# Attention scores read from PSUM by the top-32 search, and expert sums on ScalarE and GpSimd

## The chip, the cores and the metric

The kernel runs on one core of one Trainium2 chip. The metric is the device time of one execution in microseconds (us); the time before is the median of three runs. The core has TensorE (PE in the profile, its weight loads PEld), VectorE (DVE), ScalarE (ACT), GpSimd (POOL) and the queue engine SyncE (SP). Each takes its instructions strictly in the order in which they were issued, so an instruction that waits holds all those behind it on its engine.

## What is computed

Attention that keeps the 32 largest scores of every row, and behind it a mixture of four experts on every token.

```python
scores = q @ k.T / 8                       # 2 batches x 8 heads, 576 x 576, 64 deep
kth    = 32nd largest score of each row
attn   = exp(scores - max) where scores >= kth else 0
attn  /= attn.sum(-1) + 1e-9
x      = concat over heads(attn @ v)       # 1152 tokens x 512
p      = domain_probs / (domain_probs.sum(-1) + 1e-9)
out    = sum over e of p[:, e] * (relu(x @ w1[e]) @ w2[e])     # 512 -> 1024 -> 512
```

All is float32. The matmuls get near that precision by splitting each operand into two float16 parts, HI and LO, and adding three products.

## The kernel before

The 1152 rows are cut into ten tiles: per batch four of 128 rows and one rest of 64. The 64-row rest of batch 0 comes first. A unit is one tile and one head (in a rest tile a pair of heads), so there are 72 units, numbered 0 to 71 here: 4, then 8 for each full tile, then 4.

What a unit does, in order:

- `emit_qk` (L596): four matmuls on PE give 128 x 576 scores in two PSUM banks, 288 columns each (`ps0`, `ps1`).
- `emit_scopy` (L617): ScalarE copies both halves into an SBUF tile `s`, of which there are four. The banks are then free for the next unit.
- `topk_op` (L623): seven steps on VectorE find the 32 largest. MAX8 gives the eight largest; MATCH_REPLACE overwrites them with a very small number in the work tile `w`; four rounds. The first search and the first replacement read `s`, the others `w`. Between consecutive steps of one unit stand steps of the next.
- `emit_exp` (L666): ScalarE writes exp of `s` into `w`, behind the last search.
- `emit_mask` (L670): for units 0 to 19 (tiles marked `d` in `MASKS`) VectorE does compare and multiply in one instruction (L675). For units 20 to 71 (`b`) VectorE writes the comparison as float16 over `s` (L679) and GpSimd multiplies it into `w` (L681).
- `emit_a` (L683): ScalarE makes the HI part and GpSimd the LO part, both in the tile `s`; `emit_at` transposes them by a DMA; `emit_av` (L702) multiplies by V into a PSUM bank `av`, one for four heads.
- `emit_x_half` (L736) divides by the row sums on VectorE, and `emit_x_end` makes the float16 parts of x.

The experts (`moe`, L821) run per tile: for each expert and each half of the 1024 hidden columns, 48 or 96 first-layer matmuls into a bank `m1`, the float16 parts of the hidden rows on ScalarE and GpSimd (`h_hi`, `h_lo`, which pass through one SBUF tile `hf`), and 12 or 24 second-layer matmuls (L915) into a bank `m2`, which gathers one expert's whole output. `evac` (L918) scales that output by the token's weight and sums the experts in `acc`: ScalarE writes the first expert's, VectorE adds the others (L935). The eight PSUM banks are two for scores, two `av`, two `m1`, two `m2`. Weights are loaded, scaled and split once, during the first 160 us.

Nothing in the loops sets the order: each step is an event with places taken from the table `ISSUE`, one number for each part of the step, and the events are issued by rising place (L1131). The table is written out by hand or by a planner, and decides where every instruction stands on every engine.

## Time and profile before

| | us |
|---|---|
| median of 3 runs | 584.38 |
| lowest and highest | 582.45, 586.53 |
| the profiled execution: its own time | 585.51 |
| its span, first to last instruction | 583.3 |
| busy: PE, DVE | 518.1, 491.5 |
| busy: ACT, POOL | 376.4, 363.2 |

The profile is of one execution, whose time is 2.2 us longer than its span. Starts in the timeline count from the start of the span. Busy time of PE says little on how full it is, since matmuls overlap in the records: a row of 0.22 us can be followed by the next after 0.06 us. What tells is the distance from start to start.

### The profile page before, as it was taken

The page shows a single profiled execution, that of the slowest core. Times are in us where ns is not written, and L with a number is a line of the kernel's source. Part 1 is how long each engine was busy: PE and PEld are TensorE (multiplying, and loading weights), DVE is VectorE, ACT ScalarE, POOL GpSimd, SP SyncE. Part 2 cuts the span into 40 slices and gives each one's busy share as a digit, 9 for nine tenths or more (in the row PEclk, how much of TensorE's full clock was granted, in tenths as well). Part 3 has the DMA queues.
Part 4 walks back from the last instruction along what each step waited for, and adds up shares of the span by engine and source line. Part 5 has one row for each costly group of instructions (what it writes and reads, how often), then busy time and mean ns, then how long its engine had stood idle before and what let it go on. Part 6 is the DMA issues. An engine that isn't in the chain of part 4 may idle for free. (4 is left out here: it accounts for less than half of the span.)

```text
span 583.3 us, 16478 instructions
## 1 busy us (share of the span) xinstructions
PE 518.1 (89%) x6676; PEld 390.3 (67%) x6676; DVE 491.5 (84%) x1066; ACT 376.4 (65%) x755; POOL 363.2 (62%) x387
## 2 busy tenths in 40 slices
PE   6669462658899999999899999999999999999996
PEld 3459461646577687776678775876878686677683
DVE  2888998899999999999989999999999988780122
ACT  3878988898774755677787876566565646443301
POOL 1344997898765656768777876667575747435300
PEclk9768665757899999999999999999999999999999
DMA  7999877234224353445465454234323314212210
GB/s 180 360 241 341 129 188 228 44 74 72 49 49 78 65 81 71 89 81 124 105 108 114 88 99 96 51 81 78 60 62 63 74 26 81 39 21 39 43 30 10
DMA packets 140459, 57.05 MB, mean 98 GB/s; under 512 B 128864, under 2 KB 132064, under 8 KB 140384
## 3 DMA queue, kind: packets, MB, share of 16 engines
q1 hardware_dynamic: 138016, 53.38, 43.3%
q10 hardware_dynamic: 2368, 2.62, 1.4%
q8 instruction: 52, 0.85, 0.6%
q14 instruction: 23, 0.19, 0.1%
HBM read 24.14 MB, written 2.36 MB: 45 GB/s over the span
## 5 line engine op out<-in xcount | busy, mean ns | idle before, releaser
L876 PE MATMUL m<-xt,w 128*128 128x128 f16 (+1 forms) x1280 | 203.0, 217 | 1.3 <-POOL w L420 1.3
L915 PE MATMUL m<-w,h 128*128 128x512 f16 (+1 forms) x960 | 197.5, 383 | 0.0
L874 PE MATMUL m<-xt,w 128*128 128x128 f16 (+1 forms) x1120 | 182.2, 217 | 2.4 <-DVE h L897 1.5
L875 PE MATMUL m<-xt,w 128*128 128x128 f16 (+1 forms) x1120 | 182.0, 217 | 0.0
L633 DVE MAX8 m<-w 128x8 f32<-128x576 f32 x216 | 159.6, 752 | 2.8
L915 PEld LDWEIGHTS <-h 128*128 128x128 f16 (+1 forms) x960 | 84.1, 101 | 90.2 <-issue 2.6
L876 PEld LDWEIGHTS <-w 128*128 128x128 f16 x1280 | 126.1, 100 | 1.5 <-POOL w L420 1.5
L874 PEld LDWEIGHTS <-w 128*128 128x128 f16 x1120 | 110.4, 100 | 4.4 <-DVE h L897 1.7
L875 PEld LDWEIGHTS <-w 128*128 128x128 f16 x1120 | 110.4, 100 | 2.9 <-issue 1.0
L635 DVE MATCH_REPLACE8 w<-m,w 128x576 f32<-128x576 f32 x144 | 106.6, 742 | 0.0
L894 POOL TENSOR_TENSOR h<-hf,h 128x512 f16<-128x512 f32 x64 | 75.1, 1173 | 48.7 <-ACT h L885 29.7
L691 POOL TENSOR_TENSOR s<-w,s 128x512 f16<-128x512 f32 x68 | 78.7, 1159 | 36.6 <-ACT s L689 23.6
L681 POOL TENSOR_TENSOR w<-w,s 128x576 f32<-128x576 f32 x52 | 67.1, 1292 | 46.7 <-DVE s L679 43.6
L668 ACT ACTIVATE w<-s,nb,es 128x576 f32<-128x576 f32 x68 | 58.7, 865 | 28.5 <-DVE m L633 25.0
L620 ACT ACTIVATE s<-ps 128x288 f32<-128x288 f32 x144 | 51.1, 405 | 39.1 <-PE ps L613 14.8
L689 ACT ACTIVATE s<-w 128x576 f16<-128x576 f32 x68 | 46.2, 681 | 43.7 <-POOL w L681 36.4
L633 DVE MAX8 m<-s 128x8 f32<-128x576 f32 x72 | 53.9, 748 | 15.1 <-ACT s L620 15.0
L891 ACT ACTIVATE hf<-m 128x512 f32<-128x512 f32 x64 | 37.9, 592 | 31.5 <-PE m L876 15.9
L885 ACT ACTIVATE h<-m 128x512 f16<-128x512 f32 x72 | 42.1, 590 | 24.9 <-PE m L876 23.0
L729 PE MATMUL av<-vt,at 128*128 128x65 f16 (+1 forms) x1008 | 41.8, 199 | 15.6 <-DMA at<-s 15.6
L729 PEld LDWEIGHTS <-at 128*128 128x128 f16 (+1 forms) x1008 | 38.3, 103 | 23.9 <-DMA at<-s 18.1
L635 DVE MATCH_REPLACE8 w<-m,s 128x576 f32<-128x576 f32 x72 | 53.4, 741 | 0.0
(156 smaller groups left out, 807.3 us busy)
## 6 DMA issues: line engine op xcount, KB each, us to landing
w<-in_moe_w_dram SPq DMA_DIRECT2D x16, 1024.0 KB, 8.8
qraw<-in_q_dram SPq DMA_DIRECT2D x8, 256.0 KB, 4.5
qb<-qa SPq DMA_DIRECT2D x16, 128.0 KB, 2.5
out_dram<-o ACTq DMA_DIRECT2D x8, 256.0 KB, 2.3
at<-s SPq DMA_TRANSPOSE x68, 3.2
vraw<-in_v_dram SPq DMA_DIRECT2D x2, 512.0 KB, 5.3
kraw<-in_k_dram SPq DMA_DIRECT2D x4, 256.0 KB, 3.2
vraw<-in_v_dram SPq DMA_DIRECT2D x4, 256.0 KB, 4.2
```

The source lines that it names most:

```text
L620: ACT.activation(st[:, hf * 288:hf * 288 + 288], ps[:, 0:288], AF.Copy)
L633: DVE.max(m, s_t[u] if r == 0 else w_t[u])
L635: DVE.match_replace(w_t[u], m, s_t[u] if r == 0 else w_t[u], NEG)
L668: ACT.activation(w_t[u], s_t[u], AF.Exp, bias=nb, scale=es)
L681: POOL.tensor_tensor(w, w, g, op=OP.mult)
L691: POOL.tensor_tensor(a[:, 640:1152], w[:, 0:512], a[:, 0:512], op=OP.subtract)
L729: PE.matmul(o, lhsT=att[:, blk, ps], rhs=r, start=(i == 0), stop=(i == len(seq) - 1))
L874: PE.matmul(o, lhsT=HI[e, 0, c][:, fc], rhs=xs(0, c), start=(c == 0), stop=False)
L875: PE.matmul(o, lhsT=HI[e, 0, c][:, fc], rhs=xs(1, c), start=False, stop=False)
L876: PE.matmul(o, lhsT=LO[e, 0, c][:, fc], rhs=xs(0, c), start=False, stop=(c == 3))
L894: POOL.tensor_tensor(h[:, 1], hf, h[:, 0], op=OP.subtract)
L915: PE.matmul(y[z * 64:z * 64 + M, :], lhsT=h_t[es, qd][:, p // 2, h0:h0 + M], rhs=w, start=(fc == 0 and p == 0), stop=(fc == 7 and p == 2))
```

## The change

The copy `emit_scopy` is gone. A unit's scores now lie in one PSUM tile of two banks, and there are two such tiles, four banks in place of two. First search, first replacement, exponential and mask read them there; the mask is one VectorE instruction for all units, so that GpSimd no longer multiplies. To make room, `av` and `m2` have one bank each in place of two. The tile `a` of the float16 parts is a tile of its own, out of three; `w` has four tiles in place of three. For tiles 1 to 5 (`p` in `EVAC`) the sums of experts move: ScalarE scales the output into `yf`, which shares the single SBUF tile of `hf`, and GpSimd adds it. The small matrix `pmat` is halved and its matmul done in two parts. The table `ISSUE` is new throughout, so that all instructions stand in another order; of it two lines are shown.

```diff
@@ -43,184 +43,175 @@
-MASKS = 'dddbbbbbbb'
-
...
+EVAC = 'dpppppdddd'
...
 ISSUE = [
-    (1, 4), (2, 6), (5, 8), (28, 31), (37, 50), (11,), (16, 17), (20, 21, 26, 34), (44, 58, 78, 95),
...
+    (1, 3), (4, 5), (10, 11), (6, 9), (18, 26), (27,), (34, 35), (38, 41, 88, 119), (45, 52, 106, 113),
...
 ]
 C_QK, C_V0, C_X, C_W1, C_W2 = 11, 14, 5, 10, 14
 
@@ -240,8 +231,8 @@
     cp = pool("const", 1)
     wp = pool("weights", 1)
     kvp = pool("kv", 1)
-    sp_ = pool("s", 4)
-    wkp = pool("wk", 3)
+    sp_ = pool("s", 3)
+    wkp = pool("wk", 4)
     atp = pool("at", 2)
     rawp = pool("raw", 2)
     hlp = pool("hl", 1)
@@ -251,10 +242,10 @@
     hfp = pool("hf", 1)
     op_ = pool("o", 2)
     stp = pool("st", 2)
-    ps_s = pool("pss", 1, space=PSUM)
-    ps_av = pool("psav", 2, space=PSUM)
+    ps_s = pool("pss", 2, space=PSUM)
+    ps_av = pool("psav", 1, space=PSUM)
     ps_m1 = pool("psm1", 2, space=PSUM)
-    ps_m2 = pool("psm2", 2, space=PSUM)
+    ps_m2 = pool("psm2", 1, space=PSUM)
 
     events, known = [], []
 
@@ -283,7 +274,7 @@
     with tc.manual_schedule(engines={getattr(mybir.EngineType, x) for x in MANUAL}):
 
         ident = cp.tile([128, 128], F32, name="ident")
-        pmat = cp.tile([128, 128], F32, name="pmat")
+        pmat = cp.tile([128, 64], F32, name="pmat")
         ones = cp.tile([128, 128], F32, name="ones")
         invk = cp.tile([128, B, H], F32, name="invk")
         invv = cp.tile([128, B, H], F32, name="invv")
@@ -526,7 +517,8 @@
         for i, (t, x) in enumerate(units):
             first_of.setdefault(t, i)
             last_of[t] = i
-        sp_t, s_t, w_t, m_t, a_t, at_t, av_t = {}, {}, {}, {}, {}, {}, {}
+        s_t, w_t, m_t, a_t, at_t, av_t = {}, {}, {}, {}, {}, {}
+        HS = S // 2
 
         qF, kF = [None], {}
 
@@ -560,18 +552,24 @@
             kF[x] = sp_.tile([128, S], F32, tag="s", name="kf")
             copy_rows(kF[x], p0, p1)
 
+        def scores():
+
+            return ps_s.tile([128, 2, 512], F32, tag="s", name="ps0")
+
+        def rows2(w):
+            return w.rearrange("p (t n) -> p t n", t=2)
+
         def emit_qk_whole(u, x):
-            sp_t[u] = []
+            p = scores()
+            s_t[u] = p[:, :, 0:HS]
             for hf in range(2):
-                ps = ps_s.tile([128, 512], F32, tag=f"s{hf}", name=f"ps{hf}")
+                ps = p[:, hf, :]
                 for z in (slice(0, 64), slice(64, 128)):
                     PE.matmul(ps[z, 0:288], lhsT=qF[0][z, x * 64:x * 64 + 64], rhs=kF[x][z, hf * 288:hf * 288 + 288],
                               start=True, stop=True)
-                sp_t[u].append(ps)
 
         def emit_a_whole(u):
             w = w_t.pop(u)
-            s_t.pop(u)
             p0, p1 = bank(ps_m1, "m1"), bank(ps_m2, "m2")[:, 0:64]
             for c in range(4):
                 PE.transpose(p0[:, c * 128:c * 128 + 128], w[:, c * 128:c * 128 + 128], ident)
@@ -599,9 +597,10 @@
                 emit_qk_whole(u, x)
                 return
             ta, tb = qt_t[t]
-            sp_t[u] = []
+            p = scores()
+            s_t[u] = p[:, :, 0:HS]
             for hf in range(2):
-                ps = ps_s.tile([128, 512], F32, tag=f"s{hf}", name=f"ps{hf}")
+                ps = p[:, hf, :]
                 ks = slice(hf * 288, hf * 288 + 288)
                 if t[2] == 64:
                     for j, src in enumerate((ta, tb)):
@@ -612,13 +611,6 @@
                     for j, src in enumerate((ta, tb)):
                         PE.matmul(ps[:, 0:288], lhsT=src[:, x, :],
                                   rhs=kt[x].rearrange("p c n -> p (c n)")[:, ks], start=(j == 0), stop=(j == 1))
-                sp_t[u].append(ps)
-
-        def emit_scopy(u):
-            st = sp_.tile([128, S], F32, tag="s", name="s")
-            for hf, ps in enumerate(sp_t.pop(u)):
-                ACT.activation(st[:, hf * 288:hf * 288 + 288], ps[:, 0:288], AF.Copy)
-            s_t[u] = st
 
         def topk_op(u, o):
             if u >= NU or u < 0:
@@ -631,8 +623,10 @@
                 w_t[u] = wkp.tile([128, S], F32, tag="w", name="w")
             if o % 2 == 0:
                 DVE.max(m, s_t[u] if r == 0 else w_t[u])
+            elif r == 0:
+                DVE.match_replace(rows2(w_t[u]), m, s_t[u], NEG)
             else:
-                DVE.match_replace(w_t[u], m, s_t[u] if r == 0 else w_t[u], NEG)
+                DVE.match_replace(w_t[u], m, w_t[u], NEG)
 
         eb_t, es_t = {}, {}
 
@@ -665,27 +659,19 @@
 
         def emit_exp(u):
             es, nb = eb_t.pop(u)
-            ACT.activation(w_t[u], s_t[u], AF.Exp, bias=nb, scale=es)
+            ACT.activation(rows2(w_t[u]), s_t[u], AF.Exp, bias=nb, scale=es)
 
         def emit_mask(u):
             thr = m_t.pop(u)[:, 31:32]
-            sc, w = s_t[u], w_t[u]
-            mode = MASKS[tiles.index(units[u][0])]
-            if mode == "d":
-                DVE.scalar_tensor_tensor(w, sc, thr, w, op0=OP.is_ge, op1=OP.mult)
-            else:
-                g = sc.bitcast(F16).rearrange("p (t n) -> p t n", t=2)[:, :, 0:S // 2]
-                sc, w = (z.rearrange("p (t n) -> p t n", t=2) for z in (sc, w))
-                (DVE if mode == "b" else POOL).tensor_scalar(g, sc, thr, None, op0=OP.is_ge)
-                yield
-                POOL.tensor_tensor(w, w, g, op=OP.mult)
+            w = rows2(w_t[u])
+            DVE.scalar_tensor_tensor(w, s_t.pop(u), thr, w, op0=OP.is_ge, op1=OP.mult)
 
         def emit_a(u):
             if units[u][0] == tiles[0]:
                 yield from emit_a_whole(u)
                 return
             w = w_t.pop(u)
-            a_t[u] = a = s_t.pop(u).bitcast(F16)
+            a_t[u] = a = sp_.tile([128, S], F32, tag="s", name="a").bitcast(F16)
             ACT.activation(a[:, 0:576], w, AF.Copy)
             yield
             POOL.tensor_tensor(a[:, 640:1152], w[:, 0:512], a[:, 0:512], op=OP.subtract)
@@ -775,7 +761,8 @@
                 ACT.activation(hl.bitcast(BF16)[:, 0:n], x, AF.Square, accum_out=ss)
 
             def cross():
-                PE.matmul(cross_t[t], lhsT=pmat, rhs=st["ss"], start=True, stop=True)
+                for z in range(2):
+                    PE.matmul(cross_t[t][z * 64:z * 64 + 64], lhsT=pmat, rhs=st["ss"], start=True, stop=True)
 
             def total():
                 ss = st["ss"]
@@ -931,6 +918,11 @@
                 if e == order[0]:
                     acc[0] = op_.tile([128, DM], F32, tag="o", name="o")
                     ACT.activation(acc[0][0:M], yz, AF.Copy, scale=c[0:M])
+                elif EVAC[tiles.index(t)] == "p":
+                    yf = hfp.tile([128, 512], F32, tag="hf", name="yf")[0:M]
+                    ACT.activation(yf, yz, AF.Copy, scale=c[0:M])
+                    yield
+                    POOL.tensor_tensor(acc[0][0:M], acc[0][0:M], yf, op=OP.add)
                 else:
                     DVE.scalar_tensor_tensor(acc[0][0:M], yz, c[0:M], acc[0][0:M], op0=OP.mult, op1=OP.add)
                 if e == order[-1]:
@@ -977,9 +969,7 @@
 
         def make_pmat():
             for z in range(2):
-                for y in range(2):
-                    POOL.tensor_copy(pmat[z * 64:z * 64 + 64, y * 64:y * 64 + 64],
-                                     ident[z * 64:z * 64 + 64, z * 64:z * 64 + 64])
+                POOL.tensor_copy(pmat[z * 64:z * 64 + 64], ident[z * 64:z * 64 + 64, z * 64:z * 64 + 64])
 
         def norm_probs():
             for g, r0, n, m in ((0, 0, 128, 4), (4, 512, 64, 1), (5, S, 128, 4), (9, S + 512, 64, 1)):
@@ -1061,7 +1051,7 @@
 
         for u, (t, x) in enumerate(units):
             i = 10 * u
-            for what, fn in (("qk", emit_qk), ("scopy", emit_scopy), ("nb", emit_nb), ("exp", emit_exp),
+            for what, fn in (("qk", emit_qk), ("nb", emit_nb), ("exp", emit_exp),
                              ("mask", emit_mask), ("a", emit_a), ("at", emit_at)):
                 at(i + P[what + "_0" if t == tiles[0] and what != "at" else what], fn, u)
             at(i + P["av_first" if t == tiles[0] else "av_2" if u < P["av_n"] else "av"], emit_av, u)
```

Three places in the order. Names with numbers are buffers: `m` the eight largest, `w` the work tile, `s` the copy of the scores, `ps0` the scores in PSUM, `m2` an expert's output.

VectorE in the middle of the program before, at the first search of unit 42 and the masks of units 40 (`s_4827`) and 41 (`s_4926`):

```order
L633 MAX m_5170<-s_5144 128x8
L635 MATCH_REPLACE w_5176<-m_5170,s_5144 128x576
L679 TENSOR_SCALAR s_4827<-s_4827,m_4887 128x2x288
L281 RECIPROCAL qi_5059<-qps_5061 128x1
L633 MAX m_4981<-w_4997 128x8
L633 MAX m_5170<-w_5176 128x8
L635 MATCH_REPLACE w_5176<-m_5170,w_5176 128x576
L935 SCALAR_TENSOR_TENSOR o_4490<-m2_4983,pf_4005,o_4490 128x512
L633 MAX m_5170<-w_5176 128x8
L679 TENSOR_SCALAR s_4926<-s_4926,m_4981 128x2x288
L277 TENSOR_SCALAR kpt_5284<-m2_5235 128x2
L633 MAX m_5292<-s_5287 128x8
```

The same engine there now; `ps0_4838` are the scores of unit 41, `ps0_5002` of unit 42, `ps0_5127` of unit 43:

```order
L272 RECIPROCAL invv_115<-kps_4922 128x2
L625 MAX m_5007<-w_5009 128x8
L629 MATCH_REPLACE w_5009<-m_5007,w_5009 128x576
L667 SCALAR_TENSOR_TENSOR w_4845<-ps0_4838,m_4843,w_4845 128x576
L625 MAX m_5007<-w_5009 128x8
L272 RECIPROCAL invv_115<-kps_4779 128x2
L629 MATCH_REPLACE w_5009<-m_5007,w_5009 128x576
L268 TENSOR_SCALAR kpt_5135<-m2_5121 128x2
L625 MAX m_5007<-w_5009 128x8
L625 MAX m_5159<-ps0_5127 128x8
```

Before, the mask of unit 41 stood just ahead of the first search of unit 43, and each read its own SBUF tile. Now it reads the PSUM tile into which the scores of unit 43 go next, and between this mask and that search stand two searches, a replacement and two short instructions.

VectorE at the end of attention before, where `s_8750` are the scores of unit 71 and `s_8412` those of unit 69:

```order
L633 MAX m_8753<-s_8750 128x8
L635 MATCH_REPLACE w_8755<-m_8753,s_8750 128x576
L633 MAX m_8753<-w_8755 128x8
L635 MATCH_REPLACE w_8755<-m_8753,w_8755 128x576
L633 MAX m_8753<-w_8755 128x8
L635 MATCH_REPLACE w_8755<-m_8753,w_8755 128x576
L635 MATCH_REPLACE w_8661<-m_8659,w_8661 128x576
L633 MAX m_8659<-w_8661 128x8
L679 TENSOR_SCALAR s_8412<-s_8412,m_8479 128x2x288
L679 TENSOR_SCALAR s_8564<-s_8564,m_8659 128x2x288
L633 MAX m_8753<-w_8755 128x8
L679 TENSOR_SCALAR s_8750<-s_8750,m_8753 128x2x288
```

And now, where `ps0_8221` are the scores of unit 69 and `ps0_8415` those of unit 71:

```order
L625 MAX m_8332<-w_8349 128x8
L732 TENSOR_SCALAR r_8390<-av_8132 128x4
L733 RECIPROCAL r_8390<-r_8390 128x4
L737 TENSOR_TENSOR r_8390<-r_8390,invv_115 128x4
L738 TENSOR_TENSOR x_8070<-av_8132,r_8390 128x256
L667 SCALAR_TENSOR_TENSOR w_8349<-ps0_8221,m_8332,w_8349 128x576
L268 TENSOR_SCALAR xpt_8424<-xss_8409 128x1
L270 TENSOR_SCALAR xps_8425<-xpt_8424 128x1
L927 SCALAR_TENSOR_TENSOR o_7986<-m2_8357,pf_7595,o_7986 128x512
L625 MAX m_8459<-ps0_8415 128x8
```

The mask of unit 69 has moved from behind three of the last unit's rounds to ahead of its first search.

ScalarE in the middle before, with the two copies of the scores of unit 40 (`s_4827`) and unit 41 (`s_4926`); `hf` and `h` are hidden rows of an expert:

```order
L418 ACTIVATE vt0_139<-vraw_4715 128x5x64
L620 ACTIVATE s_4827<-ps0_4801 128x288
L620 ACTIVATE s_4827<-ps1_4804 128x288
L891 ACTIVATE hf_4889<-m1_4725 128x512
L418 ACTIVATE vt1_140<-vraw_4715 128x5x64
L668 ACTIVATE w_4674<-s_4545,nb_4834,es1_4807 128x576
L789 ACTIVATE x_4239<-x_4239,xps_4831 128x512
L791 ACTIVATE xhl_4791<-x_4239 128x512
L891 ACTIVATE hf_4908<-m1_4838 128x512
L620 ACTIVATE s_4926<-ps0_4896 128x288
L620 ACTIVATE s_4926<-ps1_4899 128x288
```

And now, at a sum of experts (`yf_4767`):

```order
L878 ACTIVATE hf_4743<-m1_4641 128x512
L761 ACTIVATE xhl_4746,xss_4747<-x_4257 128x512
L872 ACTIVATE h_4755<-m1_4641 128x512
L428 ACTIVATE kt6_137,kss_4762<-kraw_4691 128x320
L675 ACTIVATE a_4765<-w_4614 128x576
L923 ACTIVATE yf_4767<-m2_4715,pf_3827 128x512
L428 ACTIVATE kt7_138,kss_4762<-kraw_4691 128x320
L662 ACTIVATE w_4702<-ps0_4628,nb_4704,es1_4490 128x576
```

The pairs of copies (L620) are gone, and a scaling of an expert's output (L923) stands between the steps of the units.

## Rows read from the trace of the kernel before

**Rows 1.** The page, part 1: busy us (share of the span) and instructions.

```profile
PE 518.1 (89%) x6676; PEld 390.3 (67%) x6676; DVE 491.5 (84%) x1066; ACT 376.4 (65%) x755; POOL 363.2 (62%) x387
```

**Rows 2.** The windows view, three stretches: busy us of each engine, PEclk, DMA.

```profile
20.00:160.00 140.00, 94.33 (x1257) 77.06 (x1258) 127.49 (x281) 119.97 (x203) 106.83 (x80) 0.70 0.69 166
160.00:500.00 340.00, 334.55 (x4206) 251.66 (x4204) 326.46 (x704) 221.46 (x482) 230.71 (x265) 1.00 0.41 79
500.00:583.30 83.30, 78.45 (x1153) 55.10 (x1149) 28.71 (x60) 24.44 (x48) 23.93 (x24) 0.99 0.14 29
```

**Rows 3.** The page, part 4: the chain that ended last, by engine.

```profile
DVE 21%; PE 18%; issue 4%; POOL 3%; ACT 1%; DVEq 0%; POOLq 0%; ACTq 0%
```

**Rows 4.** Timeline of PE: start, us, what; scores of the last unit, what follows.

```profile
510.99 0.31 PE L609 MATMUL ps<-kt,qa 128*64 128x288 f16 x2
...
511.38 0.29 PE L609 MATMUL ps<-kt,qb 128*64 128x288 f16 x2
...
511.78 0.22 PE L874 MATMUL m<-xt,wx 128*128 128x128 f16 x1
...
512.28 0.22 PE L874 MATMUL m<-xt,wx 128*128 128x128 f16 x1
```

**Rows 5.** Pieces of the chain of waits: twelve second-layer matmuls; half a unit times V.

```profile
474.83 2.59 PE m L915 x12
477.42 0.44 PE av L729 x14
```

**Rows 6.** Timeline of all engines: the end.

```profile
578.49 1.53 DVE L935 SCALAR_TENSOR_TENSOR o<-m,pf,o 64x512 f32<-64x512 f32 x2 [3.65 <-PE m L915]
```

**Rows 7.** Groups of VectorE: out<-in, count, busy us, mean ns, idle before, releaser.

```profile
L679 DVE TENSOR_SCALAR s<-s,m 128x576 f16<-128x576 f32 x52 | 31.7, 611 | 10.4 <-ACT w L668 10.3
...
L675 DVE SCALAR_TENSOR_TENSOR w<-s,m,w 128x576 f32<-128x576 f32 x20 | 24.5, 1226 | 1.2 <-ACT w L668 1.2
...
L935 DVE SCALAR_TENSOR_TENSOR o<-m,pf,o 128x512 f32<-128x512 f32 x21 | 15.5, 738 | 17.0 <-ACT o L933 9.6 <-PE m L915 7.3
```

**Rows 8.** Timeline of VectorE: two masks of the first tiles.

```profile
113.11 0.81 DVE L675 SCALAR_TENSOR_TENSOR w<-s,m,w 128x576 f32<-128x576 f32 x1
...
124.05 2.21 DVE L675 SCALAR_TENSOR_TENSOR w<-s,m,w 128x576 f32<-128x576 f32 x1
```

**Rows 9.** Timeline of GpSimd at the same times.

```profile
115.63 2.13 POOL L420 TENSOR_TENSOR w<-w 128x1024 f16<-128x1024 f32 x1 [2.48 <-ACT w L418]
...
123.52 2.12 POOL L420 TENSOR_TENSOR w<-w 128x1024 f16<-128x1024 f32 x1
```

**Rows 10.** Timeline of VectorE: a replacement, then its own search, then another.

```profile
213.16 0.74 DVE L635 MATCH_REPLACE8 w<-m,w 128x576 f32<-128x576 f32 x1
...
213.94 0.76 DVE L633 MAX8 m<-w 128x8 f32<-128x576 f32 x1
...
219.42 0.74 DVE L635 MATCH_REPLACE8 w<-m,s 128x576 f32<-128x576 f32 x1
...
220.08 0.08 DVE L635 MATCH_VALUE_LOAD w<-m,w 128x8 f32 x1
```

**Rows 11.** Timeline of VectorE: first search of unit 71, mask of unit 69.

```profile
514.60 0.74 DVE L633 MAX8 m<-s 128x8 f32<-128x576 f32 x1
...
521.01 0.50 DVE L679 TENSOR_SCALAR s<-s,m 128x576 f16<-128x576 f32 x1
```

**Rows 12.** Waits of VectorE: us in total, times, longest us.

```profile
DVE m L633 <- ACT s L620: 15.0, 6, 9.8
...
DVE w L635 <- POOL s L693: 2.7, 2, 2.3
```

**Rows 13.** Timeline of PE: scores of unit 20.

```profile
155.45 0.30 PE L613 MATMUL ps<-kt,qa 128*128 128x288 f16 x1
```

**Rows 14.** Timeline of VectorE: mask of unit 18.

```profile
166.39 1.62 DVE L675 SCALAR_TENSOR_TENSOR w<-s,m,w 128x576 f32<-128x576 f32 x1
```

**Rows 15.** Groups of GpSimd: the same columns.

```profile
L681 POOL TENSOR_TENSOR w<-w,s 128x576 f32<-128x576 f32 x52 | 67.1, 1292 | 46.7 <-DVE s L679 43.6 <-DVE qps L279 1.8 <-DVE r L746 0.9
```

2 lines of the change are left out of this document (1 added, 1 removed), and 313 rows, old and new, of the table ISSUE.

## The prediction

> **What bounds the kernel now.** I read the windows first, then the chain of waits, then single engines. The windows cut the span at 160 and 500 us: in the middle stretch PE is busy 334.6 of 340 us at a granted clock of 1.00 and VectorE 326.5, while ScalarE and GpSimd have a third of the time free [rows 2]. In the first 140 us VectorE has 127 and PE only 94, at a mean granted clock of 0.70; in the last 83 PE has 78 and VectorE 29 [rows 2]. Over the span VectorE's 491.5 and PE's 518.1 lie far above the other two [rows 1], and the part of the chain that the page shares out is VectorE 21% and PE 18% against 1% of ScalarE and 3% of GpSimd [rows 3]. So two engines are full at once.
>
> PE's fullness must be checked by starts, since busy counts overlap. Nine first-layer matmuls take 0.50 us from start to start, 0.056 each [rows 4]; twelve of the second layer take 2.59, 0.216 each; 14 matmuls times V take 0.44 [rows 5]; a unit's scores take 0.5 [rows 4]. Between the scores of unit 20, at 155.45 [rows 13], and of unit 71, at 510.99 [rows 4], the order has 2688 first-layer and 696 second-layer matmuls and some 51 units: 2688 x 0.056 + 696 x 0.216 + 51 x 0.95 = 149 + 150 + 48 = 348 us of the 355.5. PE is 98% full there. Relief of ScalarE and GpSimd is therefore worth nothing by itself; what counts is how early PE reaches the scores of unit 71, and what it still has to do behind them.
>
> **The part behind the last scores.** From 510.99 to the end of the span at 583.3 are 72.3 us, PE full until the last sums at 578.49 [rows 4, 6]. In the new order 216 second-layer matmuls stand behind these scores, against 192, and equally many of the first layer: 24 x 0.216 = 5.2 us more, so 77.5. The end is the start of unit 71's scores plus 77.5.
>
> **When VectorE lets these scores start.** The new order puts them behind the mask of unit 69, whose PSUM tile they take. Ahead of the end of that mask VectorE has 281 MAX8, 210 replacements, 70 masks, 7 sums of experts and 218 short instructions. Before, ahead of the first search of unit 71, which starts at 514.60 [rows 11], it had 283, 212, 69, 24 and 222. That is nearly the same list, so I price the differences. Consecutive independent instructions overlap by 0.08 us (a replacement of 0.74 lets the next start after 0.66 [rows 10]), so durations are taken less 0.08.
> - Seventeen sums fewer (15 moved to ScalarE and GpSimd, two placed later) at 0.738 [rows 7]: -11.2. Two MAX8, two replacements and four short ones fewer: about -3.4. Sum -14.6.
> - Masks. Before, 20 of L675 took 24.5 us and 49 of L679 at 0.611 took 29.9 [rows 7], 54.4 together. The long ones are long because of GpSimd: one beside an idle GpSimd took 0.81, another, begun 0.53 us after a GpSimd subtraction, took 2.21 and ended 0.6 us behind it [rows 8, 9]. The new mask reads one operand in PSUM and one in SBUF, as L935 does, which takes 0.738 for 512 columns [rows 7]; by 576/512 that is 0.83 and the undisturbed L675 gives 0.81. I take 0.81: 70 x 0.81 = 56.7, +2.3. It divides into -8.3 for the first 20 units and +10.6 for the others, where a fast compare becomes a slow compare and multiply.
> - 140 first searches and replacements read PSUM. No row shows that. The nearest pair is L935, PSUM and SBUF, 738 for 512 columns, against the undisturbed L675, SBUF twice, 0.81 for 576 [rows 7, 8]: scaled, 0.83 against 0.81. So 0 to 0.02 us each, at most 2.8; I take 0.01, +1.4. No row shows a gain.
> - An instruction that needs the result of the one just before it starts 0.12 us later (213.94 - 213.16 = 0.78 against 0.66 [rows 10]). The new order has 170 such pairs of search and replacement, against 154: +1.9.
> - Waits that go: of 15.0 us for the copies 9.8 is the first wait of the program [rows 12], of which only the copies themselves, about 0.7, vanish; 5.2 + 0.7 = 5.9, and 2.7 for GpSimd's reads of an SBUF tile [rows 12]. Sum -8.6.
>
> So -14.6 + 2.3 + 1.4 + 1.9 - 8.6 = -17.6: the mask of unit 69 ends at 497.0, the end is at 574.6, plus whatever VectorE newly waits for.
>
> The price of PSUM is where a rule speaks against this change. The Trainium skill's Perfetto Trace Analysis, section Optimizing Scalar/DVE Operations, gives VectorE an access overhead of about 60 ns in SBUF and 125 ns in PSUM per instruction, and VectorE: DVE Perf Modes, Rules for kernel authors, advises to copy PSUM to SBUF first for many operations. By it the 140 reads would cost an estimated 140 x 0.065 = 9.1 in place of 1.4 and the end would come 7.7 us later; the pair L935 and L675 does not show such a step.
>
> **When PE gets there.** PE reaches the scores of unit 20 behind the mask of unit 18, which began at 166.39 before and took 1.62 [rows 14]. Ahead of it VectorE saves 19 masks at 0.42, two MAX8, a replacement and four short ones (10.7), and some 4 us of waits for copies, and pays 1.2 for PSUM and dependences: it ends near 154.5, no later than PE was there before (155.45). The new order has by then 144 first-layer matmuls more behind it, and between units 20 and 71 it has 2544 and 672, so 8.0 + 5.2 = 13.2 us less: 355.5 - 13.2 = 342.3, and the last scores start at 496.8, the end is at 574.3. Both chains give nearly the same, so neither engine can fall far behind the other.
>
> **What the moved work needs.** The 15 scalings go to ScalarE and the additions to GpSimd, whose multiplication of 576 columns takes 1.29 [rows 15], so 512 some 1.15; both engines have over 100 us free in the middle [rows 2]. A scaling holds `hf`, through which hidden rows pass, until GpSimd has added, and the only `m2` bank until ScalarE has read it. By the order, ten of the 45 uses of that bank have less than 1.5 us of other PE work between them and the use before; an evacuation of 0.738 [rows 7] with its two semaphores hardly fits there. One is in the first us, seven stand next to a one-column sum that VectorE reads at once, two lie between experts. At 0.3 to 0.7 for the seven and 1 for the two that is 4 to 7 us of PE, part of which falls together with a wait for scores.
>
> **The new wait.** A unit's scores wait on PE for the mask two units earlier, and everything queued on PE, expert matmuls included, waits behind them; VectorE's first search of that unit waits for the scores. By the order VectorE has a median of 1.4 us of other work between that mask and that search (0.6 at least, 4.9 at most, 70 units); scores take 0.39 + 0.29 = 0.68 us from first start to last end [rows 4]. If PE stands ready, 5 units of 70 are too tight, for under 1 us in all. If PE is behind by more than 0.7 us, VectorE stops, where it had some microseconds of reserve before. I take 2.5 us for this and the single bank together: span 577, which is 6.2 us under this execution's 583.3. The runs shown have their median at 584.4, 1.1 below the profiled execution's time, so the forecast is **578 us**.
>
> **The rivals**, in times of a run (span and 1.1).
> - *Lockstep (slower).* Two score tiles tie the two full engines together: each unit pays what one is late against the other. With 51 units behind unit 20, 0.35 us each is 18 and 0.55 is 28 us: 574.6 + 18 to 28, 594 to 604. It decides from 0.28 us a unit (14.5 us), where the time is 1% over the present. For it: both chains end within 1 us of each other, PE's work between scores comes in pieces of 0 to 13 us by the order, and nothing buffers them. Against it: the order knows the lengths, which hardly vary.
> - *The gain is spent on smaller stalls (same).* PE loses 8 us to the single bank and the new wait takes up to 6: 574.6 + 8 to 14. Or a VectorE instruction that reads PSUM loses its overlap of 0.08 us with the next [rows 10]: 140 x 0.08 = 11.2 in place of 1.4, 574.6 + 9.8 and part or all of the 2.5. Both give 584 to 590; since both engines are full, either loss shows in full. Against the second: L935 reads PSUM and its length shows no such step. I give it 0.08 of this case's 0.23. This is also the case in which the overheads of Perfetto Trace Analysis, the page of the Trainium skill cited above, would end, with an estimated 574.6 + 7.7 + 2.5 = 585; the trace bears them out little so far.
> - *Still faster.* No new wait shows, the mask no longer meets GpSimd, and GpSimd has 67 us of multiplications less [rows 15] against 17 of additions, so that short VectorE instructions with two SBUF inputs, which also stood behind it, gain 3 to 8 us: 568 to 573.
>
> **How the numbers follow.** Forecast (573 to 584) 0.36, of which 0.24 lies under the line of 578.5; same 0.23; lockstep 0.23; still faster 0.18. A measurement of this kernel can tell about 1%, that is 578.5 and 590.2. Faster: 0.24 + 0.18 = 0.42. Slower: lockstep, 0.23. Same is the rest, 0.35. The range leaves out the outer parts of the two end cases: 563 to 599.
>
> **What would show it.** Right: the mask of unit 69 ends near 500; MAX8 and replacements from PSUM last as those from SBUF, within 0.02; masks take 0.8 with little spread; PE's second layer waits for its bank no more than 7 us in all; VectorE's idle time between 160 and 500, 13.5 us now [rows 2], stays under 15. Wrong: waits of first searches on PE's scores in tens of microseconds with PE waiting for masks (lockstep); reads of PSUM 0.05 us longer or more; or PE not 8 us ahead at unit 20, because the split of the weights comes no earlier.

## The result, and the profile after

The changed kernel takes 587.78 us, median of 16 runs (584.8 to 590.0), against 583.34 for the kernel before (579.91 to 587.39): a ratio of 1.0071, 95% interval 1.0048 to 1.0094. The forecast was 578, range 563 to 599. One execution of 1313 us in a later set of runs (`after_again` below) is left out of every ratio. The time lies in the range, but it rose by 4.4 us where a fall was forecast; it also lies in the range of the rival in which the gain is spent on smaller stalls (584 to 590), whose terms are checked in the part on why the prediction was wrong.

The page of the changed kernel, part 1, answers to [rows 1]:

```profile
PE 518.7 (89%) x6680; PEld 389.3 (67%) x6680; DVE 488.3 (84%) x1051; ACT 339.1 (58%) x626; POOL 307.6 (53%) x348
```

ScalarE lost 37 us and GpSimd 56, as the change says; PE has the same work and VectorE 3 us less busy time. The windows of the changed kernel, with the columns of [rows 2]:

```profile
20.00:160.00 140.00, 95.85 (x1337) 79.87 (x1337) 129.77 (x293) 117.51 (x182) 105.30 (x87) 0.76 0.63 164
160.00:500.00 340.00, 333.20 (x4118) 247.02 (x4116) 322.71 (x685) 193.26 (x386) 183.80 (x230) 0.99 0.45 80
500.00:584.20 84.20, 79.46 (x1170) 56.02 (x1167) 28.01 (x58) 22.65 (x43) 17.50 (x18) 0.99 0.14 29
```

PE is as full in the middle as before, at a mean clock of 0.99 where it was 1.00. VectorE is not: its idle time between 160 and 500 us is 17.3 us (13.5 before), above the 15 that the prediction had named as a limit. The timeline of PE in the changed kernel shows the scores of units 20 and 71 (before: 155.45 and 510.99 [rows 4, 13]):

```profile
159.75 0.28 PE L612 MATMUL ps<-kt,qa 128*128 128x288 f16 x1 [0.18 <-DVE w L667]
...
506.86 0.31 PE L608 MATMUL ps<-kt,qa 128*64 128x288 f16 x2
```

Unit 20 comes 4.3 us later, unit 71 4.1 earlier, the end (584.2) 0.9 later than in the first profile of the kernel before. That first profile is of an execution of 585.51 us, 2.2 above the median of its kind. A second one, of another execution (581.53 us, span 579.3), has in its timeline of PE:

```profile
153.41 0.28 PE L613 MATMUL ps<-kt,qa 128*128 128x288 f16 x1 [0.60 <-ACT s L620]
...
507.04 0.31 PE L609 MATMUL ps<-kt,qa 128*64 128x288 f16 x2
```

Against this one the change has won nothing at unit 71 (506.86 against 507.04) and has lost behind it: 77.4 us to the end where there were 72.3. That is 5 us, about the 4.4 between the medians.

### The profile page after: what moved, and what is told of

Its sections match the earlier page's. It is cut to its first block, busy times and chain, and to the rows that moved or that the text cites. A ratio compares the mean times of both kernels' runs of the same rounds, so it can differ in the third digit from the quotient of the medians.

```text
span 584.2 us, 16267 instructions
## 1 busy us (share of the span) xinstructions
PE 518.7 (89%) x6680; PEld 389.3 (67%) x6680; DVE 488.3 (84%) x1051; ACT 339.1 (58%) x626; POOL 307.6 (53%) x348
## 4 chain that ended last, share of the span: by engine, by line
PE 50%; DVE 31%; DMA 7%; ACT 6%; issue 3%; SPq 1%; POOL 1%; DVEq 0%; ACTq 0%; POOLq 0%
PE m L902 22%; DVE m L625 12%; DVE w L629 7%; PE m L861 6%; PE m L863 6%; PE m L862 6%; DVE w L627 4%; DVE w L667 4%; PE ps L612 3%; PE av L715 3%; DMA at<-a 2%; DMA qa<-qhl 1%; DMA kt<-khl 1%; ACT w L406 1%; ACT w L662 1%
## 5 line engine op out<-in xcount | busy, mean ns | idle before, releaser
L677 POOL TENSOR_TENSOR a<-w,a 128x512 f16<-128x512 f32 x68 | 78.8, 1159 | 63.5 <-ACT a L675 45.1
L662 ACT ACTIVATE w<-ps,nb,es 128x576 f32<-128x576 f32 x68 | 56.3, 827 | 58.9 <-DVE m L625 56.0
L625 DVE MAX8 m<-ps 128x8 f32<-128x576 f32 x72 | 54.4, 756 | 23.7 <-PE ps L568 10.9
L667 DVE SCALAR_TENSOR_TENSOR w<-ps,m,w 128x576 f32<-128x576 f32 x72 | 58.0, 807 | 11.0 <-ACT w L662 10.8
L612 PE MATMUL ps<-kt,qa 128*128 128x288 f16 x128 | 37.0, 307 | 30.2 <-DVE w L667 22.1
L878 ACT ACTIVATE hf<-m 128x512 f32<-128x512 f32 x64 | 37.8, 591 | 31.8 <-PE m L863 16.1
L627 DVE MATCH_REPLACE8 w<-m,ps 128x576 f32<-128x576 f32 x72 | 53.8, 748 | 0.3 <-issue 0.3
L675 ACT ACTIVATE a<-w 128x576 f16<-128x576 f32 x68 | 45.9, 678 | 12.5 <-DVE w L667 8.9
L715 PEld LDWEIGHTS <-at 128*128 128x128 f16 (+1 forms) x1008 | 35.9, 99 | 12.5 <-DMA at<-a 7.6
L715 PE MATMUL av<-vt,at 128*128 128x65 f16 (+1 forms) x1008 | 39.5, 194 | 5.2 <-DMA at<-a 5.0
```

Of the source, the lines that this page charges most:

```text
L625: DVE.max(m, s_t[u] if r == 0 else w_t[u])
L627: DVE.match_replace(rows2(w_t[u]), m, s_t[u], NEG)
L662: ACT.activation(rows2(w_t[u]), s_t[u], AF.Exp, bias=nb, scale=es)
L667: DVE.scalar_tensor_tensor(w, s_t.pop(u), thr, w, op0=OP.is_ge, op1=OP.mult)
L677: POOL.tensor_tensor(a[:, 640:1152], w[:, 0:512], a[:, 0:512], op=OP.subtract)
L715: PE.matmul(o, lhsT=att[:, blk, ps], rhs=r, start=(i == 0), stop=(i == len(seq) - 1))
```

## The experiments

All runs, with the start of the scores of units 20 and 71, the span, and the number of stretches between 160 and 570 us in which PE's granted clock fell to 0.50 (from windows of 2 us). Ratios are to runs of the kernel before made beside them (their medians are 581.4 to 583.3 us). The runs named `less` and `wide` leave out work to see what it is worth; the others compute the whole result.

| run | median us | ratio, 95% interval | unit 20 | unit 71 | span | half clock |
|---|---|---|---|---|---|---|
| before, first profile | 583.34 | | 155.5 | 511.0 | 583.3 | 0 |
| b_again | 581.53 (one) | | 153.4 | 507.0 | 579.3 | 0 |
| after | 587.78 | 1.0071 (1.0048-1.0094) | 159.7 | 506.9 | 584.2 | 1 |
| after_again | 587.65 | 1.0070 (1.0036-1.0104) | 159.3 | 508.6 | 586.0 | 1 |
| a_kprep | 587.26 | 1.0059 (1.0024-1.0093) | 155.1 | 506.2 | 583.6 | 2 |
| a_kprep_m2 | 583.74 | 1.0048 (1.0013-1.0083) | 155.2 | 503.8 | 581.2 | 1 |
| a_totals | 591.39 | 1.0166 (1.0126-1.0207) | 158.9 | 509.5 | 586.9 | 0 |
| a_totals_kprep | 589.20 | 1.0130 (1.0088-1.0173) | 158.5 | 512.2 | 589.6 | 3 |
| a_three | 588.62 | 1.0113 (1.0072-1.0154) | 155.5 | 506.5 | 583.9 | 0 |
| a_filler | 591.16 | 1.0165 (1.0126-1.0204) | 158.8 | 510.4 | 587.8 | 2 |
| a_sums_dve | 602.57 | 1.0348 (1.0302-1.0393) | 157.5 | 521.9 | 599.3 | 3 |
| a_early_free | 597.88 | 1.0259 (1.0220-1.0299) | 164.9 | 518.7 | 596.1 | 1 |
| a_less_dve | 585.75 | 1.0057 (1.0027-1.0087) | 157.9 | 505.6 | 583.0 | 2 |
| a_less_pe | 584.86 | 1.0020 (0.9999-1.0040) | 160.1 | 507.2 | 584.6 | 2 |
| a_less_both | 580.28 | 0.9975 (0.9948-1.0001) | 160.7 | 502.8 | 580.2 | 2 |
| a_wide_both | 559.50 | 0.9593 (0.9534-0.9652) | 159.6 | 486.4 | 558.9 | 3 |
| b_less_dve | 579.35 | 0.9931 (0.9911-0.9950) | 153.1 | 504.0 | 576.2 | 0 |
| b_less_pe | 582.69 | 0.9996 (0.9972-1.0020) | 154.1 | 508.1 | 580.3 | 1 |
| b_less_both | 577.31 | 0.9920 (0.9887-0.9953) | 154.5 | 502.4 | 574.7 | 1 |
| b_wide_both | 565.47 | 0.9706 (0.9660-0.9753) | 155.3 | 493.6 | 561.2 | 1 |

### Both kernels once more

> The changed kernel once more, beside the three others of this call. Every theory expects its time again, ratio to the kernel before 1.005 to 1.010; the spread of the single times (some 5 us in each kernel) shows how far one profile can lie from the median, and the new trace is compared with the first: where both have the same place for a unit, the difference to before is no accident of one execution.

> The kernel before once more, for a second profile: its first was 2.2 us above the median of its runs. Every theory expects 579 to 587. If PE's granted clock stays at 1.00 between 160 and 570 again, while every profile of the changed kernel has a stretch at half clock near 300, the stretch belongs to the changed kernel and not to one execution.

The changed kernel repeats the starts of units 16 to 43 to 0.7 us and has the half clock at the same place; then one wait of 1.8 us for a transpose makes it 1.8 to 2.3 us later. The kernel before has none in either profile. Its second profile took away the ground on which my differences stood: 4 us of the first were one execution's own (among them half clock from 151 to 154 us, and waits of 0.9 and 1.1 us for transposes at 284 and 292).

### The start

```diff
+for _i, _v in {2: (5.1, 5.2), 5: (7.1,), 542: (7.2,), 6: (12.1, 12.2), 7: (15.1, 15.2, 19.1, 20.1), ...}.items():
+    ISSUE[_i] = _v     # 13 events of K, unit 1's scores, the second tile's queries, unit 4's scores
```

> The changed kernel with 13 events of the first 45 us moved in the table: the sums over K for its scale stand behind unit 0's scores and first search again, as before, so that K, the second tile's queries and unit 4's scores come earlier. Theory START (what the new order lost before unit 20 is what cancels the gain): VectorE's wait of 5.7 us before unit 4 falls below 2, the mask of unit 18 ends at 155 to 157 in place of 159.7, and the time falls by 3 to 5 us, to 583 to 585. Rival FULL (PE and VectorE are both full later on and the start is set by the splits of the weights on ScalarE and GpSimd): the wait goes, but another comes in its place before 160 us, and the time falls by less than 1.5 us.

The timeline of VectorE in the changed kernel, and then in this one, at the first search of unit 4:

```profile
44.99 0.77 DVE L625 MAX8 m<-ps 128x8 f32<-128x576 f32 x1 [5.68 <-PE ps L612]
```

```profile
40.04 0.77 DVE L628 MAX8 m<-ps 128x8 f32<-128x576 f32 x1 [1.63 <-PE ps L615]
```

START is right up to unit 20: the wait of 5.7 us fell to 1.6 and unit 20 came 4.6 earlier. Then the lead was lost again, to 0.7 us at unit 71 and 0.4 in the median, as FULL has it, but not before 160 us. Part of the loss is the clock: the windows of this kernel show PE at half clock twice, for some 7 and 3.5 us, where the changed kernel has it once for 3.4.

```profile
295.00:303.00 8.00, 6.92 (x22) 2.76 (x22) 6.43 (x16) 7.64 (x18) 5.13 (x8) 0.57 0.35 79
...
449.00:453.00 4.00, 3.92 (x15) 1.94 (x15) 3.63 (x12) 2.83 (x7) 1.31 (x2) 0.59 0.12 27
```

### The half clock near 300 us

The changed kernel has one such stretch. Its timeline of PE at the place, and the windows around it:

```profile
297.16 0.29 PE L612 MATMUL ps<-kt,qb 128*128 128x288 f16 x1
297.80 0.38 PE L434 MATMUL m<-kss,ones 128*128 128x2 f32 x2 [0.35 <-ACT yf L923]
298.52 0.35 PE L434 MATMUL m<-kss,ones 128*128 128x2 f32 x2 [0.34 <-DVE kpt L268]
299.95 4.44 PE L902 MATMUL m<-w,h 128*128 128x512 f16 x12 [1.08 <-DVE kpt L268]
...
304.72 2.75 PE L902 MATMUL m<-w,h 128*128 128x512 f16 x12
```

```profile
298.00:300.00 2.00, 0.58 (x5) 0.45 (x5) 1.97 (x7) 1.74 (x5) 1.32 (x2) 1.00 0.00 0
300.00:302.00 2.00, 2.00 (x5) 0.67 (x5) 2.00 (x5) 1.94 (x5) 1.54 (x2) 0.50 0.00 0
302.00:304.00 2.00, 2.00 (x7) 0.79 (x6) 1.97 (x7) 1.97 (x5) 1.30 (x3) 0.65 0.36 96
```

Two small sums and an expert's output want the one `m2` bank: PE waits for ScalarE's `yf`, then twice for VectorE's reading of a sum, 1.8 us in all, and then twelve second-layer matmuls take 4.44 us at the lower of the two clocks (1.2 GHz); the next twelve, at the higher one, take 2.75. Two edits tried this place, `a_totals` and `a_filler`. A third moves twelve matmuls into a wait near 447 us, where the earlier start had brought another stretch of half clock; the remaining runs combine these with the earlier start:

```diff
-                st["pt"] = bank(ps_m2, "m2")             # a_totals; a_totals_kprep and a_three contain it
+                st["pt"] = last_p[0][:, 1, 320:328]      # free columns of the newest score tile
```

```diff
+for _i, _v in {..., 1415: (1852.5,)}.items():           # a_three, a_kprep_m2: 12 matmuls ahead of unit 64's scores
```

```diff
+                for _ in range({4: 14, 5: 20}.get(calls[0], 0)):      # a_filler
+                    PE.matmul(last_p[0][:, 1, 320:448], lhsT=w, rhs=w, start=True, stop=True)
```

> The changed kernel with the small sums of K and V squares of the second batch written into free columns of the newest score tile, and not into the one bank of the second layer. In the changed kernel PE waits there at 297 to 300 us (0.64, 0.60 and 1.33 us between single matmuls: for ScalarE's reading of that bank, and for VectorE's reading of a sum), and from 300.0 to 303.4 its granted clock is 0.50. Theory CLOCK (the single bank makes PE wait in short steps, and behind them the clock falls for some 3.5 us): no stretch of half clock near 300; unit 48's scores come 3 to 4 us earlier than the changed kernel's, and the time falls by 2 to 4 us, ratio to the kernel before 1.000 to 1.004. Rival FULL (VectorE's list sets the middle part whatever PE does): PE's gain turns into longer waits for masks, and the time falls by less than 1 us.

> The same with the K sums of the start earlier as well (the edit that brought unit 20's scores from 159.7 to 155.1 and lost this again: PE ran at half clock from 295 to 303 and from 449 to 453). Theory CLOCK: the first of the two stretches is gone, unit 48 comes 6 to 8 us earlier than in the changed kernel, and the time falls by 4 to 6 us against it, ratio to the kernel before 0.996 to 1.000. Rival FULL: the time stays within 2 us of the changed kernel's, ratio above 1.003.

> Both edits, and twelve second-layer matmuls moved ahead of the scores for which PE waits 2.4 to 2.7 us at 446 to 449 us (they wait for the mask two units before). Theory CLOCK: PE fills that wait with the 2.6 us of these matmuls, no stretch of half clock between 160 and 570, and the time falls by 3 to 4 us against the run with two edits, ratio to the kernel before 0.989 to 0.994, so 577 to 580: what the prediction had forecast for the change. Rival FULL: no more than 1 us.

> The changed kernel with 34 needless matmuls of 128 columns put between the small sums near 297 us, so that PE has something to do where it waits; nothing waits less, and PE has up to 0.5 us more to do. Theory CLOCK, that the idle steps just ahead of it are what lets the clock fall: granted clock 1.00 from 297 to 305, and unit 48's scores come 1 to 1.5 us earlier than in the changed kernel; the time falls by about 1 us, which is as little as can be told. Rival: the clock falls at that place for another reason, at half clock the needless work costs another us, and unit 48 comes up to 1 us later.

> The changed kernel with the K sums of the start earlier, and with the twelve second-layer matmuls ahead of the scores for which PE waits 2.4 to 2.7 us at 447 us; the small sums stay in the second layer's bank. Theory CLOCK: the stretch of half clock at 449 to 453 that the earlier start had brought is gone, the one near 297 stays; unit 71's scores come 3 to 5 us earlier than in the changed kernel, and the time is 582 to 585. Rival BOTH (what PE gains in one place it waits for VectorE in another): unit 71's scores within 1.5 us of the changed kernel's, 586 to 588.

`a_totals` has no half clock, and is slower all the same. Its waits of PE between 160 and 508 us (us, times, longest) show where: the small sums now wait on the score tile.

```profile
PE ps L613 <- DVE w L668: 3.9, 5, 2.4
PE ps L434 <- DVE w L628: 2.0, 1, 2.0
PE ps L434 <- ACT vt L428: 1.5, 1, 1.5
PE ps L434 <- DVE kpt L268: 1.1, 1, 1.1
PE ps L434 <- DVE m L626: 1.0, 1, 1.0
```

So the edit put 5.6 us of waits in the place of 2.0 that it took: 4.1 for VectorE's reading of that tile, 1.5 for ScalarE's squares, which are the sum's own input. `a_totals_kprep` has such sums too, and three stretches of half clock; `a_three` has no half clock, starts unit 20 at 155.5, and loses the lead by unit 71 (506.5). By their times CLOCK is missed in all three, and FULL is met in the two combinations (589.20, 588.62); with the edit's own waits in them none decides the question, but two kernels without any half clock were no faster than the changed one. In `a_filler` the needless matmuls ran, and the granted clock was 0.82 from 298 to 300 and 0.50 to 306. They did not take the place of the waits, though. Its timeline of PE at the small sum and the second layer:

```profile
298.74 0.35 PE L434 MATMUL m<-kss,ones 128*128 128x2 f32 x2 [1.08 <-DVE kpt L268]
...
302.02 4.76 PE L907 MATMUL m<-w,h 128*128 128x512 f16 x12 [1.05 <-DVE kpt L268]
```

With the 0.35 for `yf` PE waits 2.5 us there, more than the 1.8 without them, and the time rose by 3.4 us, which neither theory had. So the run does not tell whether a PE kept busy would have kept its clock. `a_kprep_m2` came out as CLOCK said: no half clock at 449, unit 71 3.1 us earlier than in the changed kernel, 583.74. Two things weaken this. Its first stretch of half clock was 3.4 us long where `a_kprep` had 6.8, and with that it was 1.1 us ahead of `a_kprep` before the edited place. And its executions fall into two groups, seven at 583.0 to 584.2 and three at 586.2 to 588.1, so that its ratio's interval still overlaps that of the changed kernel. It is slower than the kernel before; no version with the change and the whole work beats that.

### Who waits for whom

```diff
-                    yf = hfp.tile([128, 512], F32, tag="hf", name="yf")[0:M]        # a_sums_dve
-                    ACT.activation(yf, yz, AF.Copy, scale=c[0:M])
+                    DVE.scalar_tensor_tensor(acc[0][0:M], yz, c[0:M], acc[0][0:M], op0=OP.mult, op1=OP.add)
                     yield
-                    POOL.tensor_tensor(acc[0][0:M], acc[0][0:M], yf, op=OP.add)
```

> The changed kernel with the 15 moved sums of experts back on VectorE, each at the place where ScalarE's scaling stood. Theory FULL, in which VectorE's list sets when unit 71's scores start: 15 x 0.738 = 11 us more of VectorE, less what PE's slack takes, so 6 to 11 us more, 594 to 599. Theory BANK (the moved sums cost PE, since ScalarE and the single SBUF tile hold the one bank of the second layer longer): PE's waits before the second layer fall, and the time rises by less than 3 us or falls.

It rose by 14.9 us, more than the 11 that VectorE got and more than FULL's range. Waits of PE between 160 and 522 us:

```profile
PE ps L612 <- DVE w L667: 10.0, 10, 2.5
PE m L902 <- DVE o L922: 5.7, 3, 2.4
PE m L434 <- DVE o L922: 1.8, 1, 1.8
```

A sum that stands in VectorE's queue holds the only `m2` bank (7.5 us), and there are two more stretches of half clock. BANK falls: with one bank it is the sums left on VectorE that cost PE.

```diff
-            DVE.scalar_tensor_tensor(w, s_t.pop(u), thr, w, op0=OP.is_ge, op1=OP.mult)       # a_early_free
+            DVE.scalar_tensor_tensor(w, w, thr, w, op0=OP.is_ge, op1=OP.mult)                # thr: its exponential
```

> The changed kernel, but the mask compares the exponentials with the exponential of the threshold (one more ScalarE instruction of one column for each unit), so that the score tile is free behind the exponential and not behind the mask. Theory LOCKSTEP (two score tiles tie PE to VectorE): PE's waits for score tiles (22 us over the span) and VectorE's first searches' waits (23.7 us) fall by a third or more, and the time falls by 3 to 6 us, to 582 to 585. Rival FULL: the waits only show which of two full engines is ahead; they move elsewhere and the time stays within 2 us; the mask then reads SBUF twice, and where it meets GpSimd it is longer than the 0.81 us of now, up to 2.2 us as in the kernel before: with 72 masks 0.1 us longer on average the time rises by up to 7 us.

The tile is free earlier, and it costs 10 us. One line of VectorE in this kernel (min, median, max ns):

```profile
L669 DVE SCALAR_TENSOR_TENSOR w<-w,m x72: 799/817/2745, 20.7 to 541.0; 128x576 f32<-128x576 f32 x72
```

and of the changed kernel, whose mask reads one operand in PSUM:

```profile
L667 DVE SCALAR_TENSOR_TENSOR w<-ps,m,w x72: 794/808/820, 20.8 to 528.8; 128x576 f32<-128x576 f32 x72
```

With both operands in SBUF 53 masks take 0.80 to 0.88 us, nearly as in the changed kernel, and 19 take 0.92 to 2.75, each of them beside a GpSimd instruction; these are 14.3 us more of VectorE, which is more than the 10 us lost. The Trainium skill's SBUF — State Buffer, section Who interferes with whom, says so: two SBUF inputs contend with a GpSimd instruction that reads SBUF, one does not. The trace agrees. LOCKSTEP is not refuted by a kernel with another loss: PE's waits for score tiles fell from 22.1 to 11.0 us, and those of first searches for scores from 23.7 to 18.6, less than the third that it had.

### Less work on one engine, on both

```diff
+            if u >= NU or u < 0 or (u in SHORT and o > 4):         # less_dve: SHORT = range(24, 64, 4)
+                return
...
+                            if c in (0, 3) or tiles.index(t) not in (3, 4, 5, 6):      # less_pe
                                 PE.matmul(o, lhsT=LO[e, 0, c][:, fc], rhs=xs(0, c), start=False, stop=(c == 3))
```

> The changed kernel, where ten units (every fourth from 24 to 60) leave out the last replacement and the last search, and take the 24th largest score as threshold: some 14.6 us less for VectorE between 180 and 460 us, nothing less for PE. Theory VECTORE (VectorE's list sets when the scores come, PE has time to spare): unit 71's scores 11 to 15 us earlier and the time lower by as much, 573 to 577. Theory PE (PE's list sets it): less than 3 us. Theory BOTH (two full engines, each with some 10 us of waits on the other): 4 to 9 us, 579 to 583.

> The changed kernel, where 256 first-layer matmuls of tiles 3 to 6 are left out (in every second part of the contraction the product with the weights' low part): some 14.3 us less for PE, nothing less for VectorE. Theory PE: the time falls by 11 to 15 us, 573 to 577. Theory VECTORE: less than 3 us, and PE's waits for masks grow by as much as was left out. Theory BOTH: 4 to 9 us; since PE then waits more, stretches of half clock may grow and take part of it back.

> The kernel before with the same ten units shortened on VectorE by some 14.6 us. What the change was to give is relief of VectorE; this is such relief without the change. Theory VECTORE: 11 to 15 us faster than before, 568 to 572. Theory PE: less than 3 us. Theory BOTH: 4 to 9 us, 574 to 579. If the gain here is much larger than the 8 us of work that the change took from VectorE have brought, the change's own waits took that away.

> The kernel before with the 256 first-layer matmuls left out, 14.3 us less for PE. The same relief of VectorE brought 4 us there. Theory BOTH: 1 to 5 us, 578 to 582, and PE's waits grow by about 10 us. Theory PE alone: 11 to 15 us.

> The changed kernel with both shortenings at once: ten units search 24 scores (14.6 us less for VectorE), and 256 first-layer matmuls are left out (14.3 us less for PE). Alone the one brought 1 to 2 us and the other 3. Theory BOTH (each engine's list fills the middle part by itself, so that only what both lose shows): 11 to 15 us below the changed kernel, 573 to 577, ratio to the kernel before 0.983 to 0.989. Rival THIRD (something else, ScalarE, GpSimd or the chain of transposes, sets the middle part): less than 5 us below, ratio above 0.998.

> The kernel before with both shortenings. Theory BOTH: 11 to 15 us faster than before, 568 to 572, ratio 0.974 to 0.981, although each alone brought 4 us or less. Rival THIRD: less than 7 us.

> The changed kernel with both shortenings spread over the whole middle part, so that they lie at the same places: every second unit from 20 to 66 searches 24 scores (24 x 1.46 = 35 us less for VectorE), and in all full tiles three of four first-layer products with the weights' low part are left out (768 x 0.056 = 43 us less for PE). Theory BOTH (PE and VectorE together set the middle part; the narrow cuts brought only 6 us since they lay at different places, and between two places where the engines meet the longer list counts): 25 to 35 us below the changed kernel, 553 to 563, ratio 0.948 to 0.965. Rival THIRD (another chain sets it): less than 15 us, above 572.

> The same in the kernel before. Theory BOTH: 25 to 35 us below it, 548 to 558, ratio 0.940 to 0.957. Rival THIRD: less than 15 us, above 568. If the changed kernel falls by clearly less than the kernel before, its two score tiles hold it back once there is room.

Relief of either engine by 14 us brings 1 to 2 us (VectorE) or 3 (PE) in the changed kernel, 4 or 0.3 in the kernel before. If one engine alone set the time, relief of that one would bring 11 to 15; neither does, in either kernel. BOTH had 4 to 9 (1 to 5 in the last run) and is too high as well: only the 4 us of `b_less_dve` come near it. What is cut comes back as waits: those of PE in `a_less_pe`, 160 to 507 us (3.2 in the changed kernel), and of VectorE in `a_less_dve`, 160 to 506 (3.9 and 3.8):

```profile
PE ps L612 <- DVE w L667: 11.5, 10, 2.4
```

```profile
DVE m L626 <- PE ps L613: 11.5, 16, 1.9
DVE w L669 <- ACT w L663: 7.2, 12, 1.9
```

Both narrow cuts together brought 7.5 us in the changed kernel (5.6 by the ratios), between the two theories, and 5.6 in the kernel before, which is THIRD's range. The wide cuts (35 and 43 us) decide for the changed kernel: 28 us off, as BOTH had it. Since they are both longer and at the same places, the runs do not tell which of the two made the narrow ones bring so little. The kernel before fell by 17.5 only, less than BOTH and more than THIRD; there the longest waits of PE (160 to 490 us) are on the transposes, which stand behind GpSimd's mask, and among the next are the copies:

```profile
PE av L731 <- DMA at<-s: 7.8, 9, 2.0
...
PE ps L614 <- ACT s L621: 3.2, 5, 1.0
```

So once PE and VectorE have room the changed kernel is the faster one, 559.5 against 565.5. By these waits the work that the change takes from ScalarE and GpSimd is then worth something; no run shows that part by itself.

The copy of the scores put back in the new order, and the moved sums alone in the old one, were not run, so what each part of the change is worth by itself is not shown.

## Why the prediction was wrong

**The step that failed is the waits of VectorE.** I took 8.6 us off for waits that go and gave 2.5 for those that come. Counting each instruction of VectorE from the end of the one before, up to the end of the mask of unit 69 (506.4; before, in the first profile, up to the first search of unit 71, 514.6):

| term | forecast | measured |
|---|---|---|
| 24 sums to 7 | -11.2 | 16.1 to 4.8: -11.3 |
| searches and replacements: fewer, PSUM, dependences | +0.5 | 357.9 to 360.2: +2.3 |
| masks | +2.3 | 49.6 to 52.0: +2.4 |
| short instructions | -0.6 | 50.7 to 49.0: -1.7 |
| idle | -8.6, later +2.5 | 40.4 to 40.4: 0 |
| sum | -17.6, with the new wait -15.1 | -8.3 |

Against the profile on which the prediction stands the work was priced right, -8.3 against -9.0. The idle time outside the first searches fell by the 8.6 that I took off (25.3 to 16.7), and came back in full at the first searches, 15.1 to 23.7. Against the second profile of the kernel before, whose first search of unit 71 starts at 510.65, idle time is the same (40.2) and the work only 4.4 us less, since its masks took 47.3 and its short instructions 49.3. The waits of VectorE over the span, against [rows 12]:

```profile
DVE m L625 <- PE ps L568: 10.9, 1, 10.9
...
DVE m L625 <- PE ps L612: 10.2, 12, 5.7
DVE r L732 <- PE av L715: 9.5, 2, 9.3
...
DVE m L625 <- PE ps L608: 2.4, 2, 1.6
```

A copy that waits for PE and a search that waits for the copy became a search that waits for PE. I had struck out the second wait with the first. Of the 8.6, 5.1 lie before unit 5: 10.9 against 9.8 at unit 0, and 5.7 against 1.7 at unit 4, which in the kernel before reads

```profile
40.38 0.76 DVE L633 MAX8 m<-s 128x8 f32<-128x576 f32 x1 [1.65 <-ACT s L620]
```

The new order makes the sums over K for its scale only behind unit 0's whole search (19.0 us on VectorE, 12.5 before), so everything of K comes later. The order showed this; I had read it at units 18 to 71 only.

**Unit 20 on PE** was forecast at 155.5 at the latest and came at 159.7, by the same 5 us; the prediction had named a PE not ahead at unit 20 as a sign of being wrong. `a_kprep` shows this cause, and also that mending it alone gives 0.4 us of time.

**PE between units 20 and 71**: forecast 342.3 us, measured 347.1. From starts of consecutive matmuls (a wait is what exceeds the usual step of its kind): in the second profile of before 344.3 of work and 9.2 of waits, after 333.9 and 13.4. The experts' matmuls are 13.2 less, as forecast, small steps 2.8 more, and the waits 4.2 longer, half clock included: before scores 5.9 (1.9), before the second layer 4.6 (2.4), the others 2 less. The bank and the new wait are thus some 6 us, which I had at 2.5 together.

**The part behind unit 71**: 77.5 forecast, 77.4 measured. **The price of PSUM**: VectorE's groups after, with the columns of [rows 7]:

```profile
L625 DVE MAX8 m<-w 128x8 f32<-128x576 f32 x216 | 160.8, 754 | 3.1
L629 DVE MATCH_REPLACE8 w<-m,w 128x576 f32<-128x576 f32 x144 | 106.8, 742 | 0.0
L667 DVE SCALAR_TENSOR_TENSOR w<-ps,m,w 128x576 f32<-128x576 f32 x72 | 58.0, 807 | 11.0 <-ACT w L662 10.8
L625 DVE MAX8 m<-ps 128x8 f32<-128x576 f32 x72 | 54.4, 756 | 23.7 <-PE ps L568 10.9 <-PE ps L612 10.2 <-PE ps L608 2.4
L627 DVE MATCH_REPLACE8 w<-m,ps 128x576 f32<-128x576 f32 x72 | 53.8, 748 | 0.3 <-issue 0.3
```

The same first searches and replacements on the page of the kernel before, from SBUF:

```profile
L633 DVE MAX8 m<-s 128x8 f32<-128x576 f32 x72 | 53.9, 748 | 15.1 <-ACT s L620 15.0
L635 DVE MATCH_REPLACE8 w<-m,s 128x576 f32<-128x576 f32 x72 | 53.4, 741 | 0.0
```

So a read of PSUM costs 8 ns more in a first search and 7 in a first replacement (forecast 10 at the middle), not the 65 that follow from the Trainium skill's Perfetto Trace Analysis, section Optimizing Scalar/DVE Operations. Nor is the overlap of 0.08 us lost, the second branch of the rival of smaller stalls: in the changed kernel the next independent instruction starts 0.66 us after a replacement that reads PSUM, as before [rows 10].

```profile
238.95 0.75 DVE L627 MATCH_REPLACE8 w<-m,ps 128x576 f32<-128x576 f32 x1
239.61 0.15 DVE L272 RECIPROCAL qi<-qps 128x1 f32<-128x1 f32 x1
```

The masks stay within 0.79 to 0.82 beside GpSimd, as forecast. GpSimd's additions took 1.27 us, not 1.15, off the path.

**Behind the failed step** stands a wrong use of a right finding. Two engines were full, I wrote, and then added up each one's list as if it hardly waited for the other (ends at 574.6 and 574.3) and took that, with 2.5 us on top, as the time. With both at 96% a saving counts only where both have it: VectorE's 4.4 us less of work, and PE's 10 us less between units 20 and 71, did not move unit 71's scores against the second profile, and the 24 matmuls moved behind it then cost their 5 us. The lockstep rival had the mechanism (waits on the two score tiles) and the wrong size (0.35 to 0.55 us a unit; PE's 4.0 more over 51 units are 0.08). The rival of smaller stalls has the right time mostly by luck: its 8 us at the single bank were 2.2, its wait for masks of up to 6 was 4.0, and it did not have the loss before unit 20. (Its estimated 585 is a span; as a time of a run it would be 586.) Baselines too: one profile, 2.2 us above its median, was 4 us above another.

What stays open is how much of the 4 us is the half clock (1.7 us of it lie on the twelve matmuls, 4.44 against 2.75), and why it falls: waits of 2.2 to 2.8 us before the scores near 450 were followed by it in seven of these runs and not in three (2.2 in the changed kernel twice, 2.4 in `a_totals`), and a wait of 2.5 us before the first layer in `a_kprep_m2` and `a_three` was not.

## What to carry to other kernels

Where two engines are both full, price a change by what it takes from both; of 14 us taken from one, 4 or less came out of the time, and only long cuts on both at the same places came out of it for the most part. When an intermediate copy is removed, its waits pass to whoever read it: carry them over before striking them out. And read a new order from its first instruction, and take two profiles of the kernel before, before forecasting a per cent.
